# Splitting the last w2 row's load by partitions, and merging the bias load, in a decode kernel for attention plus MLP

## The chip, the cores and the metric

The kernel runs on one core of a Trainium2 chip. The metric is the device time of one execution in microseconds (us). The kernel before takes 133.66 us, the median of 3 runs (133.63 to 133.71).

## The reference

One decode step for two sequences (B = 2, one token each, D = 576). A layer norm of x feeds two branches whose results are added to x:

```
xn  = layernorm(x)
A   = attention(xn): q = xn @ wq (32 heads of 128), the last W = 2048 positions of the k and v caches
      (16 kv heads, each used by 2 query heads), softmax, @ v, then @ wo
B   = MLP(xn): h = relu(xn @ w1 + b1)^2, F = 4608;  h @ w2 + b2
out = x + A + B
```

All inputs are bf16. Almost all of the time goes into reading the caches (8 loads of 2 MB each for k and for v) and the weights wq, w1, wo and w2 once.

## The kernel before, in words

The attention works in 8 units (4 groups of 4 kv heads, times 2 sequences). `load_k` and `load_v` (lines 109 to 113) load one unit's 2 MB on SP's queue into one of six buffers. `step(u)` (388) transposes a unit's k on TensorE, computes scores, softmax, and the product with v of the unit two before. `q_rows` (227) needs wq; `mlp_h` (357) needs w1 and the bias.

All large loads are issued by SP, in the program's order, and all of them run on one DMA queue: wq, k and v units, w1 (line 430), the last k and v, then at lines 437 to 443 wo, w2a, w2b and w2c. ACT issues only small loads: x at line 126 (2 rows), the first MLP bias b1 at 418 to 420, b2 at 421 (1 row), and at the end a scratch store of two rows to the output (477), which the real store at 479 overwrites. SP issues the store of the other half (480).

w2 has 4608 rows of 576. It is laid out so that each partition holds 18 rows for each of two halves, `w2_rows[0]` and `w2_rows[1]` (208). The first half is w2a. Of the second half, rows 0 to 8 are w2b and rows 9 to 17 are w2c, a tile of its own that is loaded in three transfers after all else, rows 9 to 14, 15 to 16 and 17:

```python
W2P = [(9, 15), (15, 17), (17, 18)]
for r0, r1 in W2P:
    nc.sync.dma_start(out=w2c_sb[:, (r0 - R9) * D:(r1 - R9) * D], in_=w2_rows[1, :, r0 * D:r1 * D])
```

So the last transfer of the kernel's loads has 128 rows of 1,152 bytes, 144 KB, one for each partition.

`out_acc` (216) multiplies one row of weights by the matching column of activations: two matmuls of 288 columns that accumulate in `out_ps`. Lines 459 to 474 run it over wo, w2a, w2b and w2c in the order in which they arrive; after the ninth row of the second half, three matmuls into `spin_ps` (472) that nothing reads are issued. Then ACT copies `out_ps` to `fin_sb` (478), and ACT and SP store it. Rows 9, 15 and 17 of the second half are the first that need a new w2c transfer. The matmuls are all issued through one helper, so they show as line 93.

The bias b1 is kept as 8 rows of 576 (`b1_sb`, 207). It comes in two transfers, of rows 0 to 3 and 4 to 7, and is first used by `mlp_h`, where it starts the accumulation.

Of the kernel before, what the change touches and what calls it, by code (L numbers as in the profile page):

```python
# [16 lines left out]
def kernel(  # L17
# [14 lines left out]
    nc = tc.nc  # L32
    P = 128
    B, Sq, D = A_x.shape
# [39 lines left out]
    FR = L1 // P  # L74
    assert HW == 32 * FR and QH * 2 == NC and NC * WC == 32
    W2P = [(9, 15), (15, 17), (17, 18)]
    R9 = 9
    HD = D // 2
    RO = 32 + B
    RP = 96 + B  # L80
# [11 lines left out]
    def matmul(*a, **k):  # L92
        tc.keep_in_program_order(nc.tensor.matmul(*a, **k))  # L93
# [86 lines left out]
    for t0, half, k0, n, pc in ((0, 0, 0, NK, 0), (0, 1, 0, NK, 1), (1, 0, 1, NK - 1, 1), (1, 1, 0, NK - 1, 0)):  # L180
# [11 lines left out]
                          in_=own[:].unsqueeze(2).to_broadcast([P, NC, WC]))  # L192
# [11 lines left out]
                          in_=ident[0:2 * NG4, 0:2 * NG4].rearrange("p (x g) -> p x g", g=NG4).unsqueeze(3)  # L204
                          .to_broadcast([2 * NG4, 2, NG4, B]))

    b1_sb = const.tile([2 * NG4, HW], BF16, name="b1_sb")
    w2_rows = B_w2.rearrange("(x p r) n -> x p (r n)", x=2, r=FR)


    w2c_sb = w2pool.tile([P, (FR - R9) * D], BF16, name="w2c")

    out_ps = psum.tile([RO, HD], F32, tag="out", name="out_ps")
    nc.vector.memset(out_ps[:], 0.0)

    def out_acc(lhsT, rhs, o, start=False, stop=False, acc=out_ps, base=0):
        for i in range(2):
            p = base + 32 * i
            matmul(acc[p:p + B, :], lhsT=lhsT, rhs=rhs[:, o * D + i * HD:o * D + (i + 1) * HD], start=start,
                   stop=stop, skip_group_check=True, tile_position=(0, p))  # L220
# [167 lines left out]
    def step(u):  # L388
        fin = None
        w = u - 2  # L390
        with_pv = w >= 0
        for g in range(NG):
            transposes(u, g)
            if with_pv and g == 1:
                pv(w, 0, 2)
            if with_pv and g == 2:
                pv(w, 1, 2)
                fin = pv_end(w)
            if g == TG + 1:
                scores(u, 0)  # L400
            if g == TG + 2 and fin:
                fin()
        scores(u, 1)
        softmax(u)

    def pv_all(u):
        pv(u, 0, 1)
        pv_end(u)()
# [7 lines left out]
    softmax(0)  # L416
    load_v(2)
    b1_rows = B_b1.rearrange("(x n) -> x n", n=HW)
    for i0, i1 in ((0, 4), (4, 8)):
        nc.scalar.dma_start(out=b1_sb[i0:i1, :], in_=b1_rows[i0:i1, :])  # L420
    nc.scalar.dma_start(out=xb_sb[B:B + 1, :], in_=B_b2.rearrange("(o n) -> o n", o=1))
    step(1)
    load_k(4)
# [14 lines left out]
    w2a_sb = w2pool.tile([P, FR * D], BF16, name="w2a")  # L438
    w2b_sb = kvpool.tile([P, R9 * D], BF16, tag="kv", name="w2b")
    nc.sync.dma_start(out=w2a_sb[:], in_=w2_rows[0])  # L440
    nc.sync.dma_start(out=w2b_sb[:], in_=w2_rows[1, :, 0:R9 * D])
    for r0, r1 in W2P:
        nc.sync.dma_start(out=w2c_sb[:, (r0 - R9) * D:(r1 - R9) * D], in_=w2_rows[1, :, r0 * D:r1 * D])
    step(NU - 1)
    pv_all(NU - 2)
    pv_all(NU - 1)
    pre_ps = psum.tile([RP, HD], F32, tag="sc", bufs=2, name="pre_ps")
    nc.vector.memset(pre_ps[:], 0.0)
    pre_sb = work.tile([P, HD], F32, tag="t1", name="pre_sb")
    nc.gpsimd.memset(pre_sb[:], 0.0)  # L450
# [17 lines left out]
    for r in range(FR):  # L468
        w, o = (w2b_sb, r) if r < R9 else (w2c_sb, r - R9)
        out_acc(hT_sb[:, 1, r, :], w, o, stop=(r == FR - 1))  # L470
        if r == R9 - 1:
            for _ in range(3):
                matmul(spin_ps[0:B, :], lhsT=ws[:, 0, :], rhs=wo_sb[:, 0:512], start=True, stop=True,
                       skip_group_check=True)

    fin_sb = work.tile([RO, HD], BF16, tag="fin", name="fin_sb")
    nc.scalar.dma_start(out=out2d[:, 0:HD], in_=w2b_sb[0:B, 0:HD])
    nc.scalar.copy(out=fin_sb[:], in_=out_ps[:])
# [32 lines left out]
```

## Time and profile before

| | |
|---|---|
| median of 3 runs | 133.66 us |
| the profiled execution | 133.6 us |
| its span in the profile | 131.7 us |
| granted TensorE clock, mean | 0.883 of full speed |
| TensorE matmuls (PE) busy | 84.6 us, 64% |
| VectorE (DVE) busy | 63.1 us, 48% |
| ScalarE (ACT) busy | 46.6 us, 35% |
| read from HBM | 53.62 MB, 407 GB/s over the span |
| share of the chain that ended last in DMA | 74% |

The profile follows one execution. The span is the time between the first and the last instruction that it records; the execution's own time is 1.9 us longer. Times within it are counted from the span's start. The views used below are the chain of work that ended last, the table of stretches (busy time of each engine, granted clock and DMA share in chosen windows), the DMA queues with their packets, and the waits. The DMA share is the mean over 16 DMA engines: 0.50 means that eight are busy. A row of one partition is one packet of the DMA, up to the sizes here, and each transfer ends with a 4-byte completion write on every engine that took part.

### The profile page before, as it was taken

Reading aid. Unit: us, or ns where it says so; the run is one execution under the profiler, and the core shown is the slowest. Engines: PE = TensorE matmul, PEld = TensorE weight load, DVE = VectorE, ACT = ScalarE, POOL = GpSimd, SP = SyncE. Lnnn points to the kernel's source line nnn. Section 1 sums busy time; section 2 is a strip of 40 time slices with the busy share of each in tenths; the row PEclk is TensorE's granted clock in tenths of the full one; section 3 lists DMA queues with packets and bytes.
Section 4 is the critical chain, followed back from the end, with each engine's and each line's share of the span. In section 5 each row is a group of like instructions: output and inputs, shape, how many; then the busy total and the mean of one; then the engine's idle time right before and its main releaser. Section 6 shows DMA issues by size and latency. Waiting matters only on the chain.

```text
span 131.7 us, 2025 instructions
## 1 busy us (share of the span) xinstructions
PE 84.6 (64%) x818; PEld 46.3 (35%) x818; DVE 63.1 (48%) x176; ACT 46.6 (35%) x68; POOL 4.2 (3%) x14
## 2 busy tenths in 40 slices
PE   0040767985599687699687797003919974629782
PEld 0010236553346353345353353002507631205341
DVE  6760034555447677457677496400073487560000
ACT  6700019497255185265085283200015452000101
POOL 2000000010100100100100100100010001000000
PEclk9999999999779999859999999955586899655799
DMA  4999999999999999999999999999999989899970
GB/s 118 480 419 420 418 443 418 448 418 423 445 413 438 423 443 428 413 458 413 443 423 411 458 490 403 408 431 428 413 443 418 504 381 504 382 416 403 400 286 1
DMA packets 3643, 53.74 MB, mean 408 GB/s; under 512 B 418, under 2 KB 563, under 8 KB 819
## 3 DMA queue, kind: packets, MB, share of 16 engines
q1 hardware_dynamic: 3604, 53.61, 95.6%
q8 instruction: 6, 0.10, 0.3%
q10 hardware_dynamic: 30, 0.02, 0.0%
q14 instruction: 3, 0.02, 0.0%
HBM read 53.62 MB, written 0.00 MB: 407 GB/s over the span
## 4 chain that ended last, share of the span: by engine, by line
DMA 74%; PE 15%; ACT 5%; issue 1%; SPq 1%; DVE 1%; ACTq 0%; DVEq 0%
DMA w<-in_B_w_dram 24%; DMA w2c<-in_B_w_dram 23%; DMA k<-in_A_k_cache_dram 17%; DMA wq<-in_A_wq_dram 10%; PE kT_ps L96 5%; PE h_ps L93 3%; ACT kT L273 3%; PE q_ps L93 2%; PE sc_ps L93 2%; PE o_ps L93 1%; PE out_ps L93 1%; ACT L305 1%; SPq L120 1%; DVE qrow L241 1%; ACT qrow L241 0%
## 5 line engine op out<-in xcount | busy, mean ns | idle before, releaser
L96 PE MATMUL kT_ps<-ident_f,k 128*128 128x128 f32 x256 | 39.0, 295 | 6.7 <-DMA k<-in_A_k_cache_dram 4.2
L273 ACT COPY kT<-kT_ps 128x1024 bf16<-128x1024 bf16 x32 | 31.8, 1012 | 15.3 <-PE kT_ps L96 15.3
L96 PEld LDWEIGHTS kT_ps<-ident_f,k 128*128 128x128 f32 x256 | 29.3, 149 | 21.8 <-issue 7.4
L275 DVE COPY kT<-kT_ps 128x1024 bf16<-128x1024 bf16 x32 | 21.8, 682 | 6.4 <-PE kT_ps L96 5.9
L93 PE MATMUL sc_ps<-kT,qz 128*32 128x512 bf16 x128 | 9.8, 384 | 6.1 <-DVE kT L275 5.5
L305 ACT ACTIVATE p<-sc_ps,bias 128x512 bf16<-128x512 f32 x8 | 5.5, 687 | 21.5 <-DVE gown L301 21.4
L93 PE MATMUL o_ps<-v,pT 128*32 128x512 bf16 x128 | 12.2, 466 | 0.0
L93 PE MATMUL h_ps<-w,xnT 128*4 128x288 bf16 x72 | 4.5, 442 | 8.8 <-DMA w<-in_B_w_dram 8.8
L93 PEld LDWEIGHTS <-xnT 128*4 128x4 bf16 x108 | 3.5, 117 | 18.3 <-issue 15.3
L336 DVE SCALAR_TENSOR_TENSOR o<-o_ps,in_s,o 128x128 f32<-128x128 f32 x24 | 8.2, 344 | 0.4
L308 DVE STREAM_TRANSPOSE pT<-p 128x512 bf16<-128x512 bf16 x8 | 5.7, 709 | 5.6 <-ACT p L305 5.6
L376 DVE TENSOR_TENSOR hrow<-t 100x1152 bf16<-100x1152 f32 x2 | 2.6, 1354 | 10.5 <-ACT t L374 10.5
L93 PE MATMUL q_ps<-wq,xnT 128*4 128x512 bf16 x36 | 4.2, 622 | 5.4 <-DMA wq<-in_A_wq_dram 4.0
L294 DVE TENSOR_REDUCE m<-sc_ps 128x1 f32<-128x512 f32 x8 | 5.5, 691 | 3.4 <-PE sc_ps L93 3.4
L93 PE MATMUL op_ps<-o,of_h 128*32 128x129 f32 x16 | 3.4, 299 | 4.6 <-DVE o L336 4.6
L298 POOL PARTITION_ALL_REDUCE gmax<-m x8 | 2.9, 365 | 92.2 <-DVE m L296 92.2
L93 PEld LDWEIGHTS <-qz 128*32 128x32 bf16 x128 | 2.0, 94 | 9.9 <-DVE kT L275 7.6
L334 DVE TENSOR_SCALAR o<-o_ps,in_s 128x128 f32<-128x128 f32 x8 | 2.7, 343 | 5.3 <-PE o_ps L93 5.3
L96 PE MATMUL pro_ps<-ident,xn_sb 2*128 2x2 bf16 x5 | 0.9, 181 | 6.8 <-DVE xn_sb L171 6.5
L241 ACT CAST qrow<-q_ps 100x512 bf16<-100x512 f32 x1 | 0.6, 585 | 12.1 <-DVE qrow L241 12.1
L463 ACT COPY pre_sb<-pre_ps 34x288 f32<-34x288 f32 x1 | 0.4, 393 | 12.6 <-PE pre_ps L93 12.6
L93 PE MATMUL out_ps<-wo,ws 128*2 128x288 bf16 x32 | 4.0, 441 | 1.1 <-DVE ws L352 1.1
(76 smaller groups left out, 61.4 us busy)
## 6 DMA issues: line engine op xcount, KB each, us to landing
k<-in_A_k_cache_dram SPq DMA_DIRECT2D x8, 2048.0 KB, 25.6
v<-in_A_v_cache_dram SPq DMA_DIRECT2D x8, 2048.0 KB, 22.8
w<-in_B_w_dram SPq DMA_DIRECT2D x1, 5184.0 KB
wo<-in_A_wo_dram SPq DMA_DIRECT2D x1, 4608.0 KB
wq<-in_A_wq_dram SPq DMA_DIRECT2D x1, 3584.0 KB, 12.9
w2a<-in_B_w_dram SPq DMA_DIRECT2D x1, 2592.0 KB
w2b<-in_B_w_dram SPq DMA_DIRECT2D x1, 1296.0 KB, 29.2
wq<-in_A_wq_dram SPq DMA_DIRECT2D x1, 1024.0 KB, 4.8
```

The source lines that it names most:

```text
L93: tc.keep_in_program_order(nc.tensor.matmul(*a, **k))
L96: tc.keep_in_program_order(nc.tensor.transpose(*a, **k))
L241: cp(out=qrow[:, k * QW:(k + 1) * QW].rearrange("p (i a d) -> p i a d", a=2, d=Dh), in_=q_ps[0:RB, k * QW // 2:(k + 1) * QW // 2].rearrang ...
L273: nc.scalar.copy(out=kT, in_=kT_ps[:])
L275: nc.vector.tensor_copy(out=kT, in_=kT_ps[:])
L294: nc.vector.tensor_reduce(out=m1[:], in_=sc_ps[:], axis=AX.X, op=ALU.max)
L298: nc.gpsimd.partition_all_reduce(gmax[:], m2[:], channels=P, reduce_op=ReduceOp.max)
L305: nc.scalar.activation(out=p_sb[:], in_=sc_ps[:], func=ACT.Exp, bias=bias[:, 0:1], scale=scale, accum_out=o1[:, Dh:Dh + 1])
L308: nc.vector.transpose(out=pT[:].rearrange("p j r -> p (j r)"), in_=p_sb[:])
L334: nc.vector.tensor_scalar(scalar1=in_s[:, 0:1], scalar2=None, op0=ALU.mult, **kw)
L336: nc.vector.scalar_tensor_tensor(scalar=in_s[:, k:k + 1], in1=o1[:, 0:Dh], op0=ALU.mult, op1=ALU.add, **kw)
L376: nc.vector.tensor_tensor(out=h4[:, :, k * HB:(k + 1) * HB], in0=t4, in1=t4, op=ALU.mult)
```

## The change

Row 17 of the second half is loaded in two transfers, of partitions 0 to 57 and of partitions 58 to 127. The other two w2c transfers stay as they are. The bias b1 comes in one transfer of 8 rows.

```diff
+    PE2 = 58
...
-    for i0, i1 in ((0, 4), (4, 8)):
-        nc.scalar.dma_start(out=b1_sb[i0:i1, :], in_=b1_rows[i0:i1, :])
+    nc.scalar.dma_start(out=b1_sb[:], in_=b1_rows[:, :])
...
     for r0, r1 in W2P:
-        nc.sync.dma_start(out=w2c_sb[:, (r0 - R9) * D:(r1 - R9) * D], in_=w2_rows[1, :, r0 * D:r1 * D])
+        cols = slice((r0 - R9) * D, (r1 - R9) * D)
+        for p0, p1 in ((0, PE2), (PE2, P)) if r1 == FR else ((0, P),):
+            nc.sync.dma_start(out=w2c_sb[p0:p1, cols], in_=w2_rows[1, p0:p1, r0 * D:r1 * D])
```

## The prediction

> **What bounds the kernel now.** I read the chain that ended last first, in order of time. Its tail is
>
> ```profile
> 96.48 0.42 SPq L441
> ...
> 96.95 30.81 DMA w2c<-in_B_w_dram
> 127.75 0.04 issue
> 127.80 1.36 PE out_ps L93 x18
> 129.16 0.02 issue
> 129.18 0.39 ACT fin_sb L478
> ```
>
> The columns are start, duration, what. SP issued the w2c loads at 96.95 us, the chain is in that transfer for 30.81 us, and only 18 matmuls, one eviction and the store come after it. The end is set by when the queue of loads runs dry. The next view, the table of stretches, shows how it does so:
>
> ```profile
> core 0: us, PE busy (x) PEld busy (x) DVE busy (x) ACT busy (x) POOL busy (x), PEclk, DMA share, GB/s
> 126.00:126.40 0.40, 0.40 (x12) 0.30 (x8) 0.00 (x0) 0.00 (x0) 0.00 (x0) 1.00 1.01 409
> 126.40:126.80 0.40, 0.40 (x10) 0.29 (x7) 0.00 (x0) 0.00 (x0) 0.00 (x0) 1.00 0.99 379
> 126.80:127.20 0.40, 0.40 (x6) 0.17 (x2) 0.00 (x0) 0.00 (x0) 0.00 (x0) 1.00 0.53 210
> 127.20:127.60 0.40, 0.40 (x3) 0.08 (x1) 0.00 (x0) 0.00 (x0) 0.00 (x0) 1.00 0.48 180
> 127.60:128.00 0.40, 0.24 (x5) 0.17 (x5) 0.00 (x0) 0.00 (x0) 0.00 (x0) 1.00 0.38 147
> 128.00:128.40 0.40, 0.40 (x10) 0.27 (x8) 0.00 (x0) 0.00 (x0) 0.00 (x0) 1.00 0.29 104
> 128.40:128.80 0.40, 0.40 (x10) 0.29 (x5) 0.00 (x0) 0.00 (x0) 0.00 (x0) 1.00 0.01 3
> ```
>
> Look at the second number from the right. Sixteen DMA engines are busy until 126.8, about eight from there (0.53), then six (0.38), then five (0.29). The engines stop one after another over 1.8 us, though each has carried 8 of the 128 rows of each big load. What made them uneven is in the page's list of queues:
>
> ```profile
> q1 hardware_dynamic: 3604, 53.61, 95.6%
> q8 instruction: 6, 0.10, 0.3%
> q10 hardware_dynamic: 30, 0.02, 0.0%
> q14 instruction: 3, 0.02, 0.0%
> ```
>
> q1 is SP's queue, q10 ACT's. In the trace's records of single packets (start, duration, bytes, queue) each engine's q1 packets follow one another without a gap, so an engine can be followed by its phase. The six q8 packets (16 KB, at 28.9, 48.6, 68.2, 83.0, 105.0 and 123.3 us) each put the engine they fall on about 1.41 us behind; two q14 packets of 8 KB, at 33.5 and 70.8, put theirs 0.85 and 0.55 behind. Eight engines were hit, and those are the eight still busy after 126.8.
>
> **The last transfer, engine by engine.** Rows of 1,152 B start 47 ns apart on an engine, and its completion write takes 5 to 6 ns. The sixteen completion writes of the last piece start between 126.65 and 128.48; the last lands 0.33 later, at 128.81, and row 17's first matmul starts at 128.85. The 2-row transfers tell which engines take small loads: the scratch store of L477 runs on the two engines that I call A and B. A ended its loads at 126.76, B at 127.53: B is the engine that the 70.8 us fetch hit. The first bias transfer shows four packets at once, the single-row b2 one:
>
> ```profile
> q10 hardware_dynamic: 4, 0.00, 3.8%
> ```
>
> ```profile
> q10 hardware_dynamic: 1, 0.00, 5.3%
> ```
>
> (Transfers in the windows 7.96 to 8.30 and 12.30 to 12.36.) By phases, A is in the four and in the one, B in the four.
>
> **The change, part by part.** (1) The bias. Before, four engines carry two rows and two completions: 2 x (47 + 5) = 0.104 us of lateness each. After, eight engines carry one: 0.052. So A and B gain 0.052, and four others lose 0.052. ACT issues one DMA of about 0.3 us fewer, at 4.58; it hides under the table load that runs until 5.59, so it is worth nothing. (2) SP issues one DMA more, 0.43 us, at about 100 to 106. SP has nothing behind it but the last store at 129.6, and the queue then holds over 20 us of work: nothing. The shift of the semaphores by one lets two early k/v loads go out earlier than 5.59 and 14.09, where SP waits for wq; no packet gap is seen there, so nothing again. If that cover were gone, it could cost the 0.6 us of one issue. (3) The split. Every transfer of the trace is shared in equal whole rows: 128 as 16 x 8, 4 as 4 x 1, 2 as 2 x 1. 58 is 2 x 29, so an equal share on up to 16 engines means two engines with 29 rows; 70 is 14 x 5. I take the two to be A and B, as for the other 2-engine transfers, and the fourteen to include them. Then A and B carry 34 rows in place of 8: 26 x 47 = 1.222 us, and one more completion, 0.006. The scratch store's row and completion (0.026 + 0.005) probably come in between, as B's loads now last longer: 0.031. Two engines carry nothing (-0.38), twelve carry 5 (-0.14).
>
> The sum. A: 126.76 + 1.222 + 0.006 + 0.031 - 0.052 = 127.96. B: 127.53 + 1.207 = 128.735. All others: at most 128.478 - 0.141 = 128.34, or 128.39 with the bias. So B ends last, 0.257 us after the old last, and row 17's matmul moves from 128.85 to 129.11. Behind it nothing changes. PE doesn't hide it: rows 15 and 16 end their issue at 128.77, so it waits. The profiled execution took 133.6 us (span 131.7); 133.6 + 0.26 = 133.86. The median of the runs is 0.06 above that execution, so 133.92, or +0.19%. A change under 0.2% is about what a measurement of this kernel can't tell from none; the forecast lies on that line.
>
> What isn't shown: the price of a row on an engine that carries 29 neighbours. The nearest rows, those of the last piece, say 47 ns each, with eight or fewer engines at work; the bias rows, with all sixteen at work, take the same 51 ns from start to end. Below: no row is quicker, so no gain. Above: if two engines that write side by side share one path, rows double in price while the others still run; about 25 of B's rows fall there, beside some 6 of 16 engines, 25 x 47 x 6/16 = 0.44. I take 47, the nearest, and keep 0.44 for the range. A second semaphore to wait for on PE before row 17 is hidden, because the 58-row part ends before the other on B; uncovered, it is a 17 to 38 ns instruction, as ACT's and SP's are at the end.
>
> **Rivals.** (a) B isn't late. If the fetch at 70.8 falls on another engine, B starts from 126.98 and ends at 128.18; then the others' 128.34 to 128.39 set the landing, at most 128.73, and PE is the bound: its rows 9 to 16 issue back to back, 0.122 each, from 127.80, so row 17 can't start before 128.77. Gain 0.08: 133.58. It decides at a lead of 1.21 us of B over the last engine; here it is 0.95. For it: A has 1.72, and nothing in the kernel's text fixes where a fetch falls. Against it: the fetches come with the instruction stream, which the change hardly touches. 0.20.
>
> (b) The split does not do what equal shares say: both parts use about all engines, 4 + 5 rows on the fullest, one row and one completion more, 0.053, so 133.71. For it: no transfer in the trace has a row count that isn't a small number or 128. Against it: none is shared unequally. 0.10. [...]
>
> (c) The crowded rows cost more, +0.05 to +0.44 on top: about 134.15, at most 134.36. [...] Against it: the bias rows' 51 ns. 0.20. [...]
>
> (d) The fetches fall so that the last engine is over 0.27 us earlier: 133.3. 0.05.
>
> **How the numbers follow.** The forecast as worked out has 0.45; it lies on the line, so 0.25 of it goes above 0.2% (what I left out, such as a second wait, adds time) and 0.20 below. Slower: 0.25 + 0.20 of (c) + 0.03 for fetches that fall worse, taken from (a): 0.48. Faster: 0.05. Same: 0.47. The range takes (a), (b), the forecast and most of (c): 133.5 to 134.35.
>
> **What will show it.** Right: in the table of stretches the DMA share of 128.00 to 128.80 shows one or two engines (0.06 to 0.12) until about 128.7; PE's last matmuls wait for w2c, with about 0.3 us between row 16 and row 17; the chain still ends w2c, PE, eviction. The bias shows as one window with eight q10 packets. Wrong: row 17 follows row 16 at once (a), or five engines still end together as before (b), or packets of 1,152 B take over 51 ns (c). The prediction would fail altogether if the 70-row part avoided B, or if the fetches moved.

## The result, and the profile after

The changed kernel takes 134.0 us, the median of 11 runs (133.79 to 134.2); the kernel before, on the same chip, 133.64 (133.47 to 133.8). The ratio is 1.0025, 95% interval 1.0017 to 1.0032: slower by about a quarter of a per cent. The profiled execution took 133.85 us, one of the quicker of the eleven; its span is 132.0.

The tail of the chain that ended last, of the changed kernel (start, duration, what):

```profile
96.85 31.14 DMA w2c<-in_B_w_dram
127.99 0.04 issue
128.03 1.33 PE out_ps L94 x18
129.37 0.02 issue
129.39 0.39 ACT fin_sb L480
```

It has the same links as before, and the last one starts 0.21 us later. But the first matmul that needs w2c, row 9's, already starts 0.23 later (128.03 against 127.80), and row 9 does not need the transfer that was split. The start of the w2b matmuls in the timeline shows where the delay begins (start, duration, engine and line, what, count, and the idle time just before). First the kernel before, then the changed one:

```profile
125.73 1.27 PE L93 MATMUL out_ps<-w2b,hT_sb 128*2 128x288 bf16 x18 [0.21 <-DMA w2b<-in_B_w_dram]
127.80 1.34 PE L93 MATMUL out_ps<-w2c,hT_sb 128*2 128x288 bf16 x18 [0.15 <-DMA w2c<-in_B_w_dram]
```

```profile
125.70 1.27 PE L94 MATMUL out_ps<-w2b,hT_sb 128*2 128x288 bf16 x18
128.03 1.31 PE L94 MATMUL out_ps<-w2c,hT_sb 128*2 128x288 bf16 x18 [0.42 <-DMA w2c<-in_B_w_dram]
```

w2b's matmuls start no later than before (125.70, before 125.73). From there to row 9 it is 2.33 us, before 2.07. So 0.26 us are lost while rows 9 to 14 are being loaded, a transfer that the change left alone. The table of stretches, with the columns of the table before:

```profile
core 0: us, PE busy (x) PEld busy (x) DVE busy (x) ACT busy (x) POOL busy (x), PEclk, DMA share, GB/s
126.40:126.80 0.40, 0.40 (x10) 0.26 (x6) 0.00 (x0) 0.00 (x0) 0.00 (x0) 1.00 0.77 300
126.80:127.20 0.40, 0.40 (x6) 0.17 (x2) 0.00 (x0) 0.00 (x0) 0.00 (x0) 1.00 0.58 228
127.20:127.60 0.40, 0.40 (x2) 0.08 (x1) 0.00 (x0) 0.00 (x0) 0.00 (x0) 1.00 0.52 196
127.60:128.00 0.40, 0.01 (x1) 0.00 (x0) 0.00 (x0) 0.00 (x0) 0.00 (x0) 1.00 0.51 186
128.00:128.40 0.40, 0.37 (x8) 0.26 (x8) 0.00 (x0) 0.00 (x0) 0.00 (x0) 1.00 0.33 112
128.40:128.80 0.40, 0.40 (x12) 0.29 (x8) 0.00 (x0) 0.00 (x0) 0.00 (x0) 1.00 0.04 13
```

The tail is longer: the share is 0.51 in 127.60 to 128.00, before 0.38. PE does next to nothing in that stretch (0.01 us, before 0.24). At the end the share is 0.04, less than one engine in the mean, so one engine is alone for a short time only.

The records of single packets and of landings say where the time goes. Rows 9 to 14 come as packets of 6,912 B, rows 15 and 16 as 2,304 B, row 17 as 1,152 B. In the kernel before, all 128 packets of 6,912 B but one take 262 ns, all of 2,304 B 93 ns, all of 1,152 B 51 ns. In the changed kernel five of the first kind take 268 to 341 ns from 126.67 on, twelve of the second 95 to 120, three of the third 54 to 64. I call the sum of what packets of these three sizes take over their usual time the packet excess: 4 ns before, 303 ns after.

The excess is spread over several engines, so it explains only a part of row 9's delay. From the end of the last w2b packet to the end of the last packet of rows 9 to 14 it is 2.15 us, before 2.08. The larger part comes behind that packet: it ends at 127.43 (before 127.38), and the last completion of rows 9 to 14 lands at 127.99 (before 127.76). That is 0.56 us from packet to landing, before 0.38. What holds a completion back there, the trace does not show.

The split does what equal shares said. The completions of the 58-row part land from two engines (128.19 and 128.80), those of the 70-row part from fourteen. B posts the last completion of all loads, at 128.60; it lands at 129.01, and row 17 starts at 129.06. PE had finished issuing row 16 at 129.01.

### The profile page after: what moved, and what is told of

Its sections match the earlier page's. It is cut to its first block, busy times and chain, and to the rows that moved or that the text cites. A ratio compares the mean times of both kernels' runs of the same rounds, so it can differ in the third digit from the quotient of the medians.

```text
span 132.0 us, 2025 instructions
## 1 busy us (share of the span) xinstructions
PE 84.8 (64%) x818; PEld 47.9 (36%) x818; DVE 63.2 (48%) x176; ACT 46.7 (35%) x68; POOL 4.2 (3%) x14
## 4 chain that ended last, share of the span: by engine, by line
DMA 75%; PE 16%; ACT 4%; SPq 2%; issue 1%; DVE 1%; ACTq 0%
DMA w<-in_B_w_dram 25%; DMA w2c<-in_B_w_dram 24%; DMA k<-in_A_k_cache_dram 17%; DMA wq<-in_A_wq_dram 10%; PE kT_ps L97 6%; PE h_ps L94 3%; PE q_ps L94 2%; ACT kT L274 2%; PE sc_ps L94 2%; PE out_ps L94 1%; ACT L306 1%; PE qT_ps L97 1%; PE o_ps L94 1%; SPq L121 1%; DVE qrow L242 1%
## 5 line engine op out<-in xcount | busy, mean ns | idle before, releaser
L97 PE MATMUL kT_ps<-ident_f,k 128*128 128x128 f32 x256 | 39.5, 299 | 7.3 <-DMA k<-in_A_k_cache_dram 5.9
L97 PEld LDWEIGHTS kT_ps<-ident_f,k 128*128 128x128 f32 x256 | 30.4, 152 | 21.0 <-issue 10.2
L94 PE MATMUL o_ps<-v,pT 128*32 128x512 bf16 x128 | 11.2, 433 | 0.0
```

The lines of the kernel that those rows point to most:

```text
L97: tc.keep_in_program_order(nc.tensor.transpose(*a, **k))
```

## The experiments

Each run was timed in five rounds (e12 in one) beside the kernel before on the same chip. Ratios are to that kernel, with the 95% interval. "To row 9" is the time from the start of w2b's matmuls to the start of row 9 in the run's own profile, "landing" the time from the end of the last packet of rows 9 to 14 to the last landing of that transfer, and the packet excess is counted as above. All runs but e2 and the kernel before have the merged bias. e6, e8, e10 and e12 stand in the text alone.

| run | what differs from before | ratio | to row 9, us | landing, us | excess, ns |
|---|---|---|---|---|---|
| before | | 1 | 2.07 | 0.38 | 4 |
| changed | bias merged, row 17 split 58 / 70 | 1.0025 (1.0017 to 1.0032) | 2.33 | 0.56 | 303 |
| e1_bias_only | bias merged | 1.0004 (0.9995 to 1.0012) | 2.11 | 0.35 | 2 |
| e2_split_only | split 58 / 70 | 1.0013 (1.0004 to 1.0023) | 2.20 | 0.50 | 219 |
| e4_own_rows | 58 rows replaced by scratch in two partitions | 1.0023 (1.0013 to 1.0032) | 2.37 | 0.56 | 281 |
| e5_a_only | split 31 / 1 / 96 | 1.0020 (1.0012 to 1.0029) | 2.42 | 0.60 | 1253 |
| e3_halves | split 64 / 64 | 1.0032 (1.0020 to 1.0044) | 2.37 | 0.55 | 561 |
| e7_16_112 | split 16 / 112 | 1.0034 (1.0023 to 1.0044) | 2.40 | 0.58 | 965 |
| e9_two_engines_end | unsplit, 38 rows more on A and B | 1.0003 (0.9994 to 1.0011) | 2.07 | 0.44 | 4 |
| e11_four_pieces | unsplit, one 128-row transfer more | 1.0002 (0.9994 to 1.0011) | 2.09 | 0.36 | 14 |

**The parts of the change, each alone.** The first run keeps the old row 17 and has only

```diff
-    for i0, i1 in ((0, 4), (4, 8)):
-        nc.scalar.dma_start(out=b1_sb[i0:i1, :], in_=b1_rows[i0:i1, :])
+    nc.scalar.dma_start(out=b1_sb[:], in_=b1_rows[:, :])
```

> The kernel before with the bias b1 in one transfer and row 17 in one transfer of 128 rows. Both theories (late B: engine B ends last because it carries 26 more rows; crowding: the 58 rows that two engines write to partitions which other engines fill in the usual share slow those engines' packets) say no change: 133.55 to 133.75, ratio 0.9995 to 1.0005. If the bias is the cause, some +0.2 to +0.35 us. The trace should show eight bias packets at about the same time, and the last w2c packets at 51 ns.

It measured 133.73 beside 133.69, a ratio whose interval holds 1. The bias isn't the cause. The second has the split and the two bias transfers.

> The split of row 17 alone, the bias in two transfers as before. Late B: B is 0.05 us later than with the merged bias, so 134.0 to 134.1. Crowding: as the changed kernel, 133.95 to 134.05. If the bias is the cause, 133.6 to 133.7.

It measured 133.94: slower, by less than the whole change, but the two intervals overlap. Its packets are lengthened in the same way. The split is the cause; whether the bias adds a little to it is open.

**Is it B, or the crowding?** Theory "late B" is the forecast's sum: B carries 26 more rows and ends last. Its rival is (c) of the prediction: engines slow each other where they write to each other's places. Counting alone puts at least 42 of the 58 rows there, since A and B together have 16 of the 128 rows of a whole transfer. Two runs were to part them. In one, the 58 rows are not loaded; six rows of scratch, about 36 KB for each of two engines, go to partitions 0 and 4 in their place (whose places those are, no trace shows):

```diff
+    nc.gpsimd.memset(w2c_sb[0:PE2, (FR - 1 - R9) * D:], 0.0)
...
+            if p1 == PE2:
+                for s0, s1 in ((0, UE), (UE, 2 * UE), (2 * UE, 2 * UE + 1728)):
+                    sk = kvpool.tile([P, UE], BF16, tag="kv", name=f"scr_{s0}")
+                    nc.sync.dma_start(out=sk[0:8:4, 0:s1 - s0], in_=wq_p[0:2, s0:s1])
...
```

> [...] The 70 rows stay. Late B: B's time is the same, so the time stays at +0.2 to +0.35 us over the kernel before (133.85 to 134.0). Crowding: the w2c packets of the other engines keep their 262, 93 and 51 ns, row 9 starts no later than in the kernel before, and only what is left of B's lateness stays, +0.0 to +0.12 (133.6 to 133.76).

It measured 134.02, about what late B said. But B did not set the end: row 17 follows row 16 at the ordinary pace of 0.12 us. And the packets did not keep their times, as I had taken for granted: row 9 was 0.30 late, with nine lengthened packets that start in 126.63 to 127.83. So something other than the 58 rows of A and B crowds; the 70-row part was still there. The other run takes B out of the matter:

```diff
-        for p0, p1 in ((0, PE2), (PE2, P)) if r1 == FR else ((0, P),):
+        for p0, p1 in ((0, 31), (31, 32), (32, P)) if r1 == FR else ((0, P),):
```

> Row 17 in three transfers: partitions 0 to 30 (31 is prime, so one engine, A), partition 31 (A), and 32 to 127 (16 engines, 6 rows each). A carries 38 rows in place of 8, +1.41 us, and its lead over the last engine was 1.72; all others carry 2 rows fewer. Late B: nobody is late, B gains 0.09, so no loss and up to 0.08 of gain: 133.55 to 133.65. [...]

It measured 133.92, and here late B fails: no engine was to be late, and the time grew by 0.2%, as crowding would have it. Its packet excess is the largest of all, and row 9 is 0.35 later than in the kernel before. Both misses have one thing in common: a part of 70 or 96 rows that is shared over many engines, though not as 128 rows are.

**Which crowding?** The third theory, share crowding, says that any part not shared as 128 rows are makes engines write in each other's places. No trace here shows which partitions an engine writes, so the places are inferred from the counts. Splits that change no engine's load are its test.

```diff
-    PE2 = 58
+    PE2 = 64
```

> The changed kernel split at 64 in place of 58: both parts go over 16 engines, 4 rows each, so every engine carries the same 8 rows as before and one completion write more. Three theories now: late B (A and B end last), two-engine crowding (the 58 rows of A and B slow the others' packets), and share crowding (any part that is not shared as 128 rows are, 8 to an engine in the usual places, slows the w2c packets of the late engines once the early engines reach it). Late B and two-engine crowding: no change, 133.65 to 133.78 (ratio within 0.0005). Share crowding: +0.1 to +0.3 us, w2c packets above 262 and 93 ns while early engines are in the halves, row 9 later.

```diff
-    PE2 = 58
+    PE2 = 16
```

> The changed kernel split at 16: 16 rows as 1 for each of 16 engines and 112 rows as 7 each. Late B and two-engine crowding: no change, 133.65 to 133.78. Share crowding: +0.1 to +0.3 us, with packets over 262 and 93 ns as in the halves.

They measured 134.10 and 134.04: slower by about as much as the change or more (the intervals overlap), with every engine carrying, by equal shares, its old 8 rows. Late B and two-engine crowding had said no change. The timeline of the halves:

```profile
125.82 1.27 PE L94 MATMUL out_ps<-w2b,hT_sb 128*2 128x288 bf16 x18 [0.60 <-DMA w2b<-in_B_w_dram]
128.19 1.34 PE L94 MATMUL out_ps<-w2c,hT_sb 128*2 128x288 bf16 x18 [0.46 <-DMA w2c<-in_B_w_dram]
```

The wait for w2c is 0.46 us, before 0.15, and it stands ahead of row 9, which no half belongs to. I read it as early engines being in the halves while late ones still load rows 9 to 14; the w2c packets of this run have 561 ns of excess.

A control has one transfer more without a partial one:

```diff
-    W2P = [(9, 15), (15, 17), (17, 18)]
+    W2P = [(9, 15), (15, 16), (16, 17), (17, 18)]
```

> A control: one w2c transfer more, but each with all 128 partitions: rows 15 and 16 come as two transfers of 128 rows of 1,152 B in place of one of 2,304 B, row 17 whole, the bias merged. Each engine pays 8 x (2 x 47 - 89) + 6 = 46 ns. Share crowding: +0.03 to +0.08 us and no packet over 262, 93 or 51 ns. If a further transfer is itself the cost: +0.3 us as with the halves.

It measured 133.79 beside 133.72. A further transfer alone doesn't do it.

**What A and B do by themselves.** Here row 17 is whole, and 38 rows go ahead of it into a scratch tile on two engines:

```diff
+        if r1 == FR:
+            nc.sync.dma_start(out=scr[0:38, :], in_=w2_rows[1, 0:38, r0 * D:r1 * D])
```

> The kernel with the merged bias and row 17 in one transfer of 128 rows, and ahead of it an extra load of row 17 of partitions 0 to 37 into a scratch tile: 38 rows are 2 x 19, so A and B carry 19 rows more (0.90 us). B would end at 127.53 + 0.90 - 0.05 = 128.38, still ahead of the last engine (128.48). Late B: no change to +0.05. Two-engine crowding: +0.1 to +0.25 us, slow w2c packets while A writes, row 9 later. Share crowding: no change, no slow packets.

It measured 134.46, ratio 1.0060 (1.0048 to 1.0072), but that says nothing on the question. The scratch tile was placed among the first ones and moved all later tiles by 1,152 B per partition, and 796 of the 2,048 packets of 16 KB then took 614 to 624 ns; in the kernel before 2 did. The stretch of 30 to 75 us, of this run and then of the kernel before:

```profile
30.00:75.00 45.00, 35.49 (x305) 20.18 (x305) 27.93 (x68) 22.02 (x29) 1.46 (x4) 0.92 1.01 426
```

```profile
30.00:75.00 45.00, 35.50 (x306) 19.75 (x309) 27.84 (x71) 21.10 (x28) 1.83 (x5) 0.92 1.01 429
```

The engines are as busy and move less, 426 in place of 429 GB/s, long before the extra load. The run was made again with the tile behind all others:

> The extra 38-row load of A and B again, with its scratch tile placed behind all other tiles, so that no other tile moves (in the run before it moved all later tiles by 1,152 B per partition, and 805 of the 2,048 packets of 16 KB took 614 to 622 ns in place of 611). If moved tiles made most of that loss, the 16 KB packets are at 611 again. Late B: no change to +0.05 us. Two-engine crowding: +0.1 to +0.25, w2c packets of the late engines over 262 and 93 ns while A and B write. [...]

It measured 133.72 beside 133.72. Packets of 16 KB are at 611 again, none of w2c is lengthened, and row 9 has its old distance:

```profile
125.79 1.27 PE L94 MATMUL out_ps<-w2b,hT_sb 128*2 128x288 bf16 x18 [0.52 <-DMA w2b<-in_B_w_dram]
127.87 1.35 PE L94 MATMUL out_ps<-w2c,hT_sb 128*2 128x288 bf16 x18 [0.16 <-DMA w2c<-in_B_w_dram]
```

So in this tail two engines may write 19 rows each to partitions 0 to 37 at no cost that shows, as long as B's lead covers them (B ended at 128.25, the last engine at 128.49). Other partitions weren't tried. Share crowding in its wide form is thereby wrong: these 38 rows aren't shared as 128 rows are either. What is left of it is a part that is shared over many engines.

**A late B by itself.** The 58-row load goes early, ahead of k 4, and row 17 stays whole:

```diff
     load_v(2)
+    nc.sync.dma_start(out=scr[0:58, :], in_=w2_rows[1, 0:58, 0:D])
```

> The kernel with the merged bias, row 17 in one transfer of 128 rows, and an extra 58-row load into a scratch tile early in the kernel, ahead of k 4: A and B are 1.37 us later from there on and nothing else changes at the end. Late B by itself: B ends its loads at about 127.53 + 1.37 - 0.05 = 128.85, 0.37 after the old last one, and all w2c transfers wait for it, so +0.3 to +0.45 us: 134.0 to 134.15. If B's lateness does not set the end, no change. No slow packets at the end by either crowding.

It measured 135.42, ratio 1.0133 (1.0120 to 1.0147), again with moved tiles (852 long packets of 16 KB). With the scratch tile behind the others:

> The extra 58-row load early in the kernel again, its scratch tile behind all others. A and B are later from about 48 us on. At 47 ns a row B would be 1.37 us later and end its loads 0.37 after the old last engine; the rows took 55 to 106 ns in the run before, which would make it 1.6 to 2.5 later: +0.3 to +1.5 us by late B. If the rest of the earlier loss came from the moved tiles, the other fourteen engines now end as in the kernel before.

It measured 134.60, ratio 1.0058 (1.0045 to 1.0071). The last engine now lands its completions 0.48 us after the next one (129.56 and 129.09 for row 17), row 9 waits for it, and row 9 starts 0.74 later than in the kernel before. So here an engine that was late did set the end, once its lead was used up.

That leaves 0.26 us of the 0.74. The other engines are already that much later at the end of wo, and their packets show where. A and B load the 58 rows from 47.38 to 49.02, sixteen of them in 56 to 132 ns in place of 51. Between 48.13 and 49.75, thirty packets of 16 KB take 638 ns or more in place of 611; spread over 16 engines, and without what a fetch adds to one of them, that is some 0.3 us for each. In the kernel before, only a fetch lengthens a packet in that stretch; the run with moved tiles has the same group of long packets, 48.15 to 50.12. So here, with all sixteen engines at work, a load on two engines alone did slow the others. Why these 58 rows slow the others and the 38 rows of the tail do not (more rows, other partitions, more engines at work), no run tells apart.

**The paths themselves.** My guess was that engines share paths that belong to the partitions they write. The last run puts the halves where they are large, into w2a, so that this would show:

```diff
-    nc.sync.dma_start(out=w2a_sb[:], in_=w2_rows[0])
+    for p0 in (0, 64):
+        nc.sync.dma_start(out=w2a_sb[p0:p0 + 64, :], in_=w2_rows[0, p0:p0 + 64])
```

> w2a (2.6 MB, rows of 20,736 B) in two transfers of 64 partitions each, both over 16 engines with 4 rows each; everything else as in the kernel before with the merged bias. [...] If the cause lies on the reading side or in the number of transfers, packets stay near 771 and the time within +0.5 us.

It measured 144.33 (two runs), ratio 1.0792 (1.0746 to 1.0838), 10.6 us more than the kernel before. Its table of stretches:

```profile
116.00:118.00 2.00, 0.61 (x2) 0.26 (x3) 0.97 (x4) 0.00 (x0) 0.00 (x0) 0.50 0.81 166
118.00:120.00 2.00, 0.96 (x20) 0.56 (x23) 0.00 (x0) 0.00 (x0) 0.00 (x0) 0.50 1.05 218
120.00:122.00 2.00, 2.00 (x44) 1.17 (x40) 0.00 (x0) 0.00 (x0) 0.00 (x0) 0.55 1.07 238
122.00:124.00 2.00, 0.51 (x20) 0.15 (x8) 0.00 (x0) 0.00 (x0) 0.00 (x0) 1.00 0.93 197
```

The last two numbers belong together. The engines are busy all the time (0.81 to 1.07) and move 166 to 238 GB/s, where the kernel before moves 347 to 487 in the same stretches. The median packet of 20,736 B takes 1,582 ns in place of 771, 2.05 times; eight such packets on an engine make some 6.5 us of the 10.6, and the rest was not followed. So in this run sixteen engines that write into 64 partitions at a time got about half the rate. The size of the load alone does not explain it: w2b, also 1.3 MB but into 128 partitions, took 389 ns per packet of 10,368 B in the kernel before, 426 GB/s over 16 engines. That they share paths that belong to the partitions written is the reading that fits; no trace shows such paths, and a cause on the reading side was not tested apart.

That the few packets of the tail are slowed for the same reason is inferred from this run, not shown.

## Why the prediction was right or wrong

**The number** was right: 133.92 forecast, 134.0 measured, inside the range; the profiled execution was forecast at 133.86 and took 133.85. That the sum meets it so closely is partly luck, as the terms below show, and the medians are 0.36 us apart where the forecast was 0.26. **The reason** was half right, and the half that I left out is at least as large.

**The tail as the bound, engine by engine**: right. Engines end one after another (the DMA share falls from 0.58 over 0.51 to 0.04 between 126.80 and 128.80), and A and B could be told by the scratch store.

**The bias costs or gains nothing that shows**: right (0.9995 to 1.0012). Eight bias packets of 1,152 B start between 7.87 and 9.01 in the changed kernel, each in 51 ns; that eight engines carry them is inferred from the count.

**58 rows on two engines, 70 on fourteen**: right, by the landings: two completions for the 58-row part (128.19 and 128.80), fourteen for the 70-row part, the last at 129.01. Rival (b) is out.

**B ends last**: right in the profile. B posted at 128.60, forecast 128.735. Of the difference, 0.03 is the scratch store, which came behind B's last row and not between its rows; 0.11 was there already when B ended rows 9 to 14, so it belongs to this execution and not to the split. B's 29 rows took 1.37 us, the 47 ns a row that the sum had. The completion then took 0.41 to land, not 0.33. Rival (a) fails too: the second 8 KB fetch, at 68.66, fell on B again.

**"All others: at most 128.34"**: here the sum failed. It took 47 ns a row and 0.14 us of gain for twelve engines, and it let PE start row 9 at 127.80 as before, so it put nothing on the transfers ahead of the split one. In their place stand lengthened packets and a later landing of rows 9 to 14; the others ended at 128.43, and row 9 came 0.23 later. The expected sign, some 0.3 us between rows 16 and 17, was not there: 0.17 (before 0.20), of which 0.12 is the ordinary pace. So PE was held up ahead of row 9 and hardly ahead of row 17.

**Rival (c)** had crowding, at the wrong place. It put the price on B's rows, and argued against it from the bias rows' 51 ns. In the tail no run shows the doubled row price behind its 0.44: B's rows kept their 47 ns (in mid-stream sixteen of 58 took 56 to 132 ns in place of 51). What is slowed is the late engines' own traffic ahead of row 17, and the shared-out part of 70 rows is enough to slow it: without the 58 rows row 9 still came 0.30 late, splits that load no engine more cost 0.32% and 0.34%, and 38 extra rows on A and B cost nothing that shows. In mid-stream, with all engines busy, 58 rows on A and B did slow the others by some 0.3 us; what the 58 rows add in the tail of the changed kernel stays open.

How the two causes combine in the changed kernel isn't settled to the last bit. In its profile both would give about the same end: PE was ready for row 17 at 129.01, B released it at 129.06. Without the crowding B would release it at about that time, at most 0.1 sooner if its completion landed in the 0.33 that the forecast took; without B's rows, crowding would still hold row 9, as the run without the 58 rows shows. A version with the 58 rows on A and B and the other 70 in their usual places wasn't tried, so late B alone in the tail is argued and not shown. The best that a split could give was 0.08 us, by PE's pace, and no run came under the kernel before.

## What to carry to other kernels

A load for part of the partitions was not a smaller load of the same kind here: where it is shared over many engines, the transfer still running ahead of it was slowed in every split tried (row 9 came 0.13 to 0.35 us later). Look at the DMA share and GB/s of a long stretch together: in the run with w2a in halves the share stayed (0.81 to 1.07) while the rate fell to about half (166 to 238, before 347 to 487). In a tail of a microsecond that view is too coarse (0.51 and 186, before 0.38 and 147); there, look at single packets and at the time from the last packet to its landing. To move work between DMA engines, keep transfers of all 128 partitions (one more of them cost nothing that shows, 1.0002) and check each engine's lead over the last one, for that lead is all there is to win.

## What the runs showed of the hardware

Instruction fetches decided which DMA engines were last. In the kernel before, six of 16 KB put their engines about 1.41 us behind, two of 8 KB 0.55 and 0.85, in a stream in which a 16 KB load packet takes 0.61.

Completions landed later by more than the packets ahead of them were lengthened. With row 17 whole, rows 9 to 14 landed 0.35 to 0.44 us after their last packet; with it split, 0.50 to 0.60; their last packet ended 2.08 us after w2b's last with it whole, 2.12 to 2.22 with it split.

Moving all large tiles by 1,152 B per partition lengthened 796 and 852 of 2,048 packets of 16 KB by 3 to 13 ns, though these packets' partitions and transfers stayed as they were. With the first of these shifts undone the loss of 0.6% was gone (1.0003); why the address matters was not tried.
